# Attention units of a fused attention, feed-forward and expert kernel: one plain float32 form, two heads per tile

## The chip, the cores and the metric

The kernel runs on one core of a Trainium2 chip. The metric is the device time of one execution in microseconds. In three runs the kernel before took 502.41, 504.73 and 507.37 us, median 504.73.

## The reference

Three layers follow each other.

1. A recurrent attention over 768 tokens, for 2 batches and 8 heads of 48 features. For every token `t`: `y = r_t (state + (u k_t) v_t)`, then `state = w * state + k_t v_t`, with a decay `w` (0.85 to 0.95) per head and feature.
2. A feed-forward over all 1536 tokens of 384 features: `elu(x @ w_in) @ w_out`, hidden width 2048; `w_in` and `w_out` come as float64.
3. A mixture of 8 experts: argmax of `x @ w_gate` picks an expert, the softmax weight of the choice scales it; up to 384 tokens per expert, each through `relu(x @ w1) @ w2` with 1024 hidden features.

Everything is compared in float32, so products are either made in plain float32 or from operands split into a high and a low float32r part (three products).

## The kernel before, in words

**Attention.** Tokens are cut into chunks of 128. A *unit* is one chunk of four heads: 24 units, numbered `u`; the halves of the heads alternate, so the state that unit `u` leaves is read by unit `u + 2`, and the last chunk of a batch leaves none. Inside a unit the recurrence becomes products: scores `k^T r` with powers of the decay multiplied into `r` and `k` (`decay_r` L290, `decay_k` L306), a mask that keeps the earlier tokens and puts the bonus of `u` on the diagonal (`bonus` L317 and L318, `diagonal` L322 and L324, `mask` L378), the result `y` from values and masked scores and from the state and `r` (`out`), and the state's update from scaled keys and values (`state`, `carry`). All products of attention are recorded under the helper's line 263.

There are two forms of a unit. Units 0 to 9 (`N_FULL = 10`) are *plain*: products of float32 operands, the tile of `r` and `k` has 48 rows and four heads side by side, a state product per head with a second product that decays the old state, and `out` lets two heads use the lower and two the upper columns of the array at the same time. The high part of `y` is copied by ScalarE (L451); the low part is left in PSUM by a product that takes the high part off, a step later, and copied by ScalarE too (`late_y`, L462 and L463). The state is carried by a copy of ScalarE (L411). Units 10 to 23 are *split*: `r`, `k`, values, scaled keys, masked scores and state are each divided into a high part (a cast by ScalarE) and a low part (a subtraction, all in the helper `sub`, L259, mostly on VectorE); the scores come in two halves that VectorE adds (`sum`, L374).

**Feed-forward.** A *pair* `q` (0 to 47) is two 128-wide hidden blocks of a group of 256 tokens: 18 products into the hidden blocks (`ff_in`, L490), ELU in steps of ScalarE and VectorE, a split, and 18 products out (`ff_out`, L529), two pairs later. The float64 weights are converted in thirds by VectorE (L203, L206, L209), cast by ScalarE (L221), and their low parts subtracted by GpSimd or VectorE (L225). The table `FILL` says how many thirds go where, for `q` from -10 to 10.

**Order.** One call of `half` is one step: the products of pair `q` and half of a unit's work. The first half of a unit has the scores and the mask, the second the result, the state and the carry. Steps run from `q = -10` to 37 with units 0 to 23, in program order on each engine from `q = 9` on (`manual_schedule`); before that a planner orders the instructions by estimated costs. Units 0 to 3 lie ahead of pair 0, units 5 to 9 beside pairs 0 to 9, units 10 to 23 beside pairs 10 to 37. `prep` makes ready the next unit in four stages. `Route` (L588 and what follows) finds the experts of a finished group and borrows the banks of the scores. From `q = 38` on there is no attention, and the experts' weights are loaded into its memory.

**Queues.** Loads of units (L85, L88), of weights, and most of the packing of `y` into the feed-forward's input (L472, two or five transfers per unit) are issued by SP in program order; a load waits for its buffer.

## Time and profile before

| | |
|---|---|
| runs | 502.41, 504.73, 507.37 us |
| span of the profiled execution | 502.5 us (first to last instruction; its own time is not listed apart from the runs) |
| TensorE busy | 449.2 us, 89% |
| VectorE busy | 363.7 us, 72% |
| ScalarE busy | 247.4 us, 49% |
| GpSimd busy | 227.1 us, 45% |
| DMA | 74.29 MB, mean 148 GB/s |
| pair 0 begins | 52.05 us |
| pair 10 begins | 120.02 us |
| pair 38 begins | 295.01 us |

Busy time is an average over stages with different limits. TensorE's products are pipelined, so the records of two neighbours overlap; the time between two starts is the price of a product, not its duration. A plain float32 product leaves two records. In the names of engines PE is TensorE, PEld its weight loads, DVE VectorE, ACT ScalarE, POOL GpSimd, SP SyncE.

### The profile page before, as it was taken

Reading aid. Unit: us, or ns where it says so; the run is one execution under the profiler, and the core shown is the slowest. Engines: PE = TensorE matmul, PEld = TensorE weight load, DVE = VectorE, ACT = ScalarE, POOL = GpSimd, SP = SyncE. Lnnn points to the kernel's source line nnn. Section 1 sums busy time; section 2 is a strip of 40 time slices with the busy share of each in tenths; the row PEclk is TensorE's granted clock in tenths of the full one; section 3 lists DMA queues with packets and bytes.
Section 4 is the critical chain, followed back from the end, with each engine's and each line's share of the span. In section 5 each row is a group of like instructions: output and inputs, shape, how many; then the busy total and the mean of one; then the engine's idle time right before and its main releaser. Section 6 shows DMA issues by size and latency. Waiting matters only on the chain. (4 is left out here: it accounts for less than half of the span.)

```text
span 502.5 us, 9335 instructions
## 1 busy us (share of the span) xinstructions
PE 449.2 (89%) x3646; PEld 432.0 (86%) x3646; DVE 363.7 (72%) x546; ACT 247.4 (49%) x430; POOL 227.1 (45%) x227
## 2 busy tenths in 40 slices
PE   2876996989998989889889999998999999999991
PEld 2554995989998989888889999997999999999991
DVE  7999799995788888888888853555656555755410
ACT  1222543546546655566456646654564655556310
POOL 8587475684477656676566442242110111011011
PEclk9875797799998999999999999998999999999997
DMA  8792555646643452222231028142646656662001
GB/s 225 224 329 78 164 200 181 192 126 218 211 140 101 151 183 87 77 85 90 69 93 43 18 64 313 64 157 97 210 162 235 254 194 233 222 238 97 31 26 30
DMA packets 26693, 74.29 MB, mean 148 GB/s; under 512 B 4098, under 2 KB 12702, under 8 KB 26640
## 3 DMA queue, kind: packets, MB, share of 16 engines
q1 hardware_dynamic: 24352, 68.27, 41.4%
q0 software_dynamic: 1792, 4.75, 2.6%
q8 instruction: 30, 0.49, 0.4%
q10 hardware_dynamic: 496, 0.59, 0.4%
q14 instruction: 23, 0.19, 0.2%
HBM read 57.00 MB, written 12.66 MB: 139 GB/s over the span
## 5 line engine op out<-in xcount | busy, mean ns | idle before, releaser
L490 PE MATMUL h<-xT,w 128*128 128x256 f32 x864 | 118.8, 289 | 0.4 <-DMA xT<-yh 0.4
L529 PE MATMUL x<-g,w 128*128 128x256 f32 x864 | 112.4, 284 | 1.1 <-DVE w L225 1.1
L490 PEld LDWEIGHTS h<-xT,w 128*128 128x128 f32 x864 | 110.2, 194 | 0.7 <-DMA xT<-yh 0.6
L529 PEld LDWEIGHTS x<-g,w 128*128 128x128 f32 x864 | 107.1, 192 | 1.8 <-DVE w L225 1.4
L512 POOL TENSOR_TENSOR g<-e,g 128x512 fp32r<-128x512 f32 x43 | 61.4, 1427 | 83.5 <-ACT g L509 83.3
L689 DVE TENSOR_TENSOR w<-raw,w 128x1536 fp32r<-128x1536 f32 x32 | 57.1, 1784 | 34.3 <-ACT w L688 32.1
L263 PE MATMUL h<-dT,w 128*128 128x256 f32 x576 | 73.4, 281 | 0.0
L263 PE MATMUL y<-w,ht 128*128 128x384 f32 x384 | 72.7, 338 | 0.0
L263 PEld LDWEIGHTS h<-dT,w 128*128 128x128 f32 x576 | 72.3, 190 | 0.0
L783 POOL DMA_INDIRECT out<-o,ds x16 | 15.6, 973 | 124.6 <-ACT o L781 122.2
L263 PEld LDWEIGHTS y<-w,ht 128*128 128x128 f32 x384 | 65.7, 188 | 0.0
L754 ACT ACTIVATE ht<-h 128x512 fp32r<-128x512 f32 x32 | 19.1, 598 | 60.1 <-PE h L263 60.0
L755 DVE SCALAR_TENSOR_TENSOR ht<-h,ht 128x512 fp32r<-128x512 f32 x32 | 22.1, 690 | 36.2 <-ACT ht L754 36.2
L688 ACT CAST w<-raw 128x1536 fp32r<-128x1536 f32 x32 | 47.3, 1477 | 0.8 <-DMA raw<-w 0.8
L509 ACT CAST g<-e 128x512 fp32r<-128x512 f32 x48 | 29.8, 620 | 33.3 <-DVE e L505 33.3
L505 DVE SCALAR_TENSOR_TENSOR e<-h,e 128x512 f32<-128x512 f32 x48 | 32.7, 681 | 17.8 <-ACT e L501 17.7
L497 ACT ACTIVATE e<-h 128x512 f32<-128x512 f32 x48 | 28.5, 594 | 14.1 <-PE h L490 13.4
L225 POOL TENSOR_TENSOR w<-f,w 128x768 fp32r<-128x768 f32 x13 | 30.6, 2357 | 10.5 <-ACT w L221 10.5
L324 POOL TENSOR_SCALAR_AFFINE_SELECT am<-dt 128x512 f32<-128x512 f32 x24 | 23.1, 964 | 27.0 <-DVE dt L322 25.2
L501 ACT ACTIVATE e<-e 128x512 f32<-128x512 f32 x48 | 30.4, 632 | 1.4
L221 ACT CAST w<-f 128x768 fp32r<-128x768 f32 x16 | 13.3, 834 | 23.9 <-DVE f L209 23.0
L206 DVE SCALAR_TENSOR_TENSOR f<-raw,f 128x768 uint32<-128x768 uint32 x16 | 23.3, 1458 | 0.1
(169 smaller groups left out, 683.5 us busy)
## 6 DMA issues: line engine op xcount, KB each, us to landing
raw<-w SPq DMA_DIRECT2D x32, 768.0 KB, 5.0
tok<-tok SPq DMA_DIRECT2D x24, 288.0 KB, 4.7
rk<-rkT SPq DMA_DIRECT2D x14, 448.0 KB, 3.6
raw<-w_in SPq DMA_DIRECT2D x8, 768.0 KB, 6.2
raw<-w_out SPq DMA_DIRECT2D x8, 768.0 KB, 4.6
disp<-zrow SPq DMA_DIRECT2D x6, 776.0 KB, 4.7
ds<-disp SPq DMA_DIRECT2D x9, 388.0 KB, 3.1
out<-zrow SPq DMA_DIRECT2D x4, 576.0 KB, 3.7
```

Source lines behind the costliest of these rows:

```text
L206: nc.vector.scalar_tensor_tensor(out=t, in0=high, scalar=0xC0000000, in1=t, op0=ALU.bitwise_and, op1=ALU.bitwise_or)
L225: (nc.vector if n in LO_V else nc.gpsimd).tensor_tensor(out=w[:, 1, o], in0=t.bitcast(F32), in1=w[:, 0, o].bitcast(F32), op=ALU.subtract)
L263: nc.tensor.matmul(out, x, y, start=start and n == 0, stop=stop and n == len(pairs) - 1, skip_group_check=True)
L490: nc.tensor.matmul(h_ps[:, j], win(d, f, a), x[:, :, d, c], start=n == 0, stop=n == 8)
L497: nc.scalar.activation(out=e, in_=hps[q], func=AF.Exp)
L501: nc.scalar.activation(out=elu[q], in_=elu[q], func=AF.Relu, bias=1.0, scale=-1.0)
L505: nc.vector.scalar_tensor_tensor(out=e, in0=hps.pop(q), scalar=0.0, in1=e, op0=ALU.max, op1=ALU.subtract)
L509: nc.scalar.copy(gt[q][:, 0], elu[q])
L512: eng("v" if q in ELO_V else "p").tensor_tensor(out=gt[q][:, 1], in0=elu.pop(q), in1=gt[q][:, 0].bitcast(F32), op=ALU.subtract)
L529: nc.tensor.matmul(o, wout(f, d, a), gg[:, c, j], start=f == 0 and n == 0 and d != 1, stop=f == 15 and n == 2, skip_group_check=True)
L688: nc.scalar.copy(w[:, 0], raw)
L689: low.tensor_tensor(out=w[:, 1], in0=raw, in1=w[:, 0].bitcast(F32), op=ALU.subtract)
```

## The change

There is one form of unit. Its operands are plain float32 throughout. A tile of `r` and `k` has 112 rows: one head in rows 0 to 47, another in rows 64 to 111, two such pairs side by side, so it is 256 columns wide instead of 512. The four score products read their operands from one row half each and write to two banks, one per row half. The state of a pair of heads lies in one tile, a head on either diagonal block; one product per pair makes its update (the blocks off the diagonal are not used), and one product per pair over 112 rows adds state times `r` to `y`. The tables of powers have four columns of 112 rows instead of eight, and the keys' table has the last power in it from the start. The old state is decayed by VectorE when it is carried, with the decay as a scalar per row, instead of by a product. The low part of `y` is a subtraction of VectorE in the same step as its high part, and packing follows at once. `r` and `k` are decayed in place; values are read where they were loaded; the buffers of loads are three deep instead of two. `decay_k` is on GpSimd for units 1 to 8, on VectorE for the others; the bonus is on VectorE for unit 0, on GpSimd for the others. The input of `r` and `k` is laid out by the host to match. Feed-forward, routing and experts are as before, and `FILL` is the same. Comments are gone.

```diff
@@ sizes and engines
-BONUS_V = (0, 3, 5, 7, 8)
-KD_V = (3, 8, 9)
-N_FULL = 10  # first attention units, multiplied in plain float32
+BONUS_V = (0,)
+KD_P = (1, 2, 3, 4, 5, 6, 7, 8)
@@ load_unit
-        n = D if u < N_FULL else KS
-        pool, kw = (first, {"name": f"rk{u}"}) if u < 4 else (att, {"tag": "rk", "name": "rk"})
-        rk_t[u] = pool.tile([n, 2, HH, C], F32, **kw)
-        nc.sync.dma_start(out=rk_t[u], in_=rkT[u, 0:n])
+        pool, kw = (first, {"name": f"rk{u}"}) if u < 4 else (att, {"tag": "rk", "name": "rk", "bufs": 3})
+        rk_t[u] = pool.tile([KS, 2, 2, C], F32, **kw)
+        nc.sync.dma_start(out=rk_t[u], in_=rkT[u])
@@ tables
-    ew = attc.tile([KS, H, C], F32, name="ew")
+    ew = attc.tile([KS, 4, C], F32, name="ew")
+    kp = attc.tile([P, 4, P], F32, name="kp")
+    e2 = first.tile([KS, 4, C], F32, name="e2")
+    for i in range(4):
+        nc.scalar.activation(out=e2[:, i], in_=ew[:, i], func=AF.Copy, scale=sq[:, 7, i:i + 1])
+    kp_ps = ps_tile(psA, "u")[:, 0:4 * KS]
+    for i in range(4):
+        nc.tensor.transpose(kp_ps[:, i * KS:(i + 1) * KS], e2[:, i], ident[0:KS, 0:KS])
+    nc.scalar.copy(kp[:, :, 0:KS], kp_ps.rearrange("p (i d) -> p i d", i=4))
...
@@ class Unit
+        def decay(self, j, on):
+            x = self.rk[:, j]
+            eng(on).tensor_tensor(out=x, in0=x, in1=ew[:, self.i2], op=ALU.mult)
         def decay_r(self):
+            self.decay(0, "v")
         def decay_k(self):
+            self.decay(1, "p" if self.u in KD_P else "v")
-        def split_r(self):
-        def split_k(self):
-        def values(self):
-        def split_kt(self):
...
         def decay_kt(self):
+            if not self.last:
+                k4 = self.tk[:, 1].rearrange("p (m q d) -> p q m d", m=2, q=2)
+                nc.vector.tensor_tensor(out=self.heads(self.kh), in0=k4, in1=self.heads(kp[:, self.i2]), op=ALU.mult)
+        def scores(self):
+            a = bank().rearrange("p (m x) -> p m x", m=2)[:, :, 0:2 * C]
+            self.a_ps = a.rearrange("p m (q t) -> p m q t", q=2)
+            for q in range(2):
+                for m in range(2):
+                    row = slice(64 * m, 64 * m + D)
+                    group(self.a_ps[:, m, q], [(self.rk[row, 1, q], self.rk[row, 0, q])])
-        def sum(self):
-        def split_a(self):
...
         def state(self):
+            self.u_ps = ps_tile(psA, "u")[0:KS, 0:4 * D].rearrange("p (q m d) -> p q m d", q=2, m=2)
+            v4 = self.tk[:, 2].rearrange("p (m q d) -> p q m d", m=2, q=2)
+            for q in range(2):
+                group(self.u_ps[:, q], [(self.kh[:, q, 0:KS], v4[:, q])])
         def carry(self):
+            for m in range(2):
+                row = slice(64 * m, 64 * m + D)
+                st = self.st[row, :, row]
+                if not self.c:
+                    nc.scalar.copy(st, self.u_ps[row, :, m])
+                    continue
+                for q in range(2):
+                    nc.vector.scalar_tensor_tensor(
+                        out=st[:, q], in0=st[:, q], scalar=sq[row, 7, 2 * self.hf + q:2 * self.hf + q + 1],
+                        in1=self.u_ps[row, q, m], op0=ALU.mult, op1=ALU.add)
-        def split_s(self):
         def out(self):
+            v = self.tk[:, 2]
+            if self.c:
+                for q in range(2):
+                    group(y_two[:, q], [(self.st[:, q, 0:KS], self.rk[:, 0, q])], start=q == 0, stop=False)
+            for q in range(2):
+                for m in range(2):
+                    h = 2 * m + q
+                    group(y_two[64 * m:64 * m + D, q], [(v[:, h * D:(h + 1) * D], self.am[:, h])],
+                          start=q == 0 and not self.c)
         def split_y_low(self):
+            nc.vector.tensor_tensor(out=self.yh[:, :, 1], in0=y_two, in1=self.yh[:, :, 0].bitcast(F32),
+                                    op=ALU.subtract)
+            self.pack()
-        def late_y(self):
@@ half, the one form that is left
-        low_y()
-        prep(n + 1, 0 if first else 1)
-        if not first and not ff:
+        if first:
+            prep(n + 1, 0)
+        elif not ff:
             prep(n + 1, 2)
...
         if x and first:
             x.scores()
-            if n - 1 in units:
-                units.pop(n - 1).late_y()
         elif x:
             x.out()
-            if n == 1:
-                key_table()
             x.state()
...
             elu_max(q)
+        if x and not first:
+            units.pop(n).split_y_low()
+        if ff:
             elu_hi(q)
...
             x.carry()
-            x.split_s()
             prep(n + 1, 3)
-    def half_split(q, n, first):
```

## Rows read from the trace of the kernel before

**Rows 1.** slices of the page: VectorE, busy tenths in 40 equal parts.

```profile
DVE  7999799995788888888888853555656555755410
```

**Rows 2.** windows: busy us (x) of PE, PEld, DVE, ACT, POOL; clock, DMA, GB/s.

```profile
0.00:52.00 52.00, 33.01 (x212) 24.09 (x212) 47.39 (x74) 12.35 (x25) 37.07 (x47) 0.77 0.70 213
52.00:120.00 68.00, 61.61 (x507) 57.84 (x506) 62.71 (x72) 31.94 (x62) 43.46 (x26) 0.90 0.56 177
120.00:295.00 175.00, 159.44 (x1475) 155.76 (x1474) 149.66 (x264) 100.89 (x204) 108.65 (x116) 0.99 0.33 105
```

**Rows 3.** TensorE's waits from 120 to 295 us: us in total, times, longest.

```profile
PE a L263 <- DVE kst L259: 7.3, 8, 2.2
PE a L588 <- DVE as L374: 2.7, 3, 1.0
PE a L263 <- ACT xr L591: 2.2, 2, 1.1
```

**Rows 4.** TensorE timeline, split unit: start us, us, instruction, [idle before].

```profile
192.32 0.51 PE L263 MATMUL u<-vh,kh 128*48 128x96 f32 x8
192.67 0.30 PE L263 MATMUL y<-r,st_s 112*48 112x128 f32 x2
...
193.90 1.28 PE L490 MATMUL h<-xT,w 128*128 128x256 f32 x9
195.92 0.71 PE L263 MATMUL a<-r,kst 112*128 112x256 f32 x4 [0.74 <-DVE kst L259]
196.47 1.22 PE L490 MATMUL h<-xT,w 128*128 128x256 f32 x9
```

**Rows 5.** TensorE's timeline, pairs with no attention beside them.

```profile
307.81 2.31 PE L490 MATMUL h<-xT,w 128*128 128x256 f32 x18
309.96 2.27 PE L529 MATMUL x<-g,w 128*128 128x256 f32 x18
312.06 2.31 PE L490 MATMUL h<-xT,w 128*128 128x256 f32 x18
```

**Rows 6.** TensorE's timeline, scores, result and state of plain units.

```profile
95.61 1.05 PE L263 MATMUL a<-r_f,k_f 128*128 128x128 f32 x8
96.42 1.31 PE L529 MATMUL x<-g,w 128*128 128x256 f32 x9
...
112.97 2.31 PE L490 MATMUL h<-xT,w 128*128 128x256 f32 x18
115.21 0.43 PE L263 MATMUL y<-r_f,st_f 128*48 128x128 f32 x4
...
116.12 0.25 PE L263 MATMUL u<-vh,kh 128*48 128x48 f32 x2
...
117.81 2.37 PE L529 MATMUL x<-g,w 128*128 128x256 f32 x18
```

**Rows 7.** windows, line 259 alone: busy us (x) of DVE and POOL.

```profile
120.00:295.00 175.00, 53.99 (x63) 7.24 (x11) 0.99 0.33 105
```

**Rows 8.** groups by shape, VectorE: busy us, mean ns, idle before.

```profile
L290 DVE TENSOR_TENSOR rk<-rk,ew 112x512 f32<-112x512 f32 x14 | 16.1, 1149 | 0.0
...
L290 DVE TENSOR_TENSOR r_f<-rk,ew 48x512 f32<-48x512 f32 x10 | 10.6, 1066 | 0.0
...
L318 DVE TENSOR_TENSOR tok<-tok 128x192 f32<-128x192 f32 x5 | 3.2, 632 | 0.0
...
L608 DVE SCALAR_TENSOR_TENSOR eq<-lg,mx,io 128x8 f32<-128x8 f32 x12 | 6.5, 578 | 0.2
...
L415 DVE TENSOR_TENSOR st_f<-u,st_f 48x192 f32<-48x192 f32 x8 | 2.8, 350 | 0.8
...
L720 DVE TENSOR_TENSOR dT<-u,dT 128x256 fp32r<-128x256 f32 x2 | 0.8, 420 | 1.0 <-ACT dT L723 1.0
```

**Rows 9.** groups by shape: ScalarE's copies of y and of the state.

```profile
L451 ACT CAST yh<-y 112x256 fp32r<-112x256 f32 x10 | 3.7, 366 | 15.6 <-PE y L263 8.4 <-DMA xT<-yh 7.1
...
L411 ACT COPY st_f<-u 48x192 f32<-48x192 f32 x8 | 2.5, 308 | 8.0 <-PE y L263 5.9 <-PE u L263 2.0
```

More of the change, by code (lines that the diff above doesn't have):

```diff
@@ L160, in bank @@
         return psA.tile([P, 1024], F32, tag="a", name="a")
-    st_s = [attc.tile([KS, HH, D], F32R, name=f"st_s{i}") for i in range(2)]
-    for i in range(2):
-        nc.gpsimd.memset(st_s[i].bitcast(F32), 0.0)
     win_t, wout_t = [], []
@@ L361, in scores @@
-        def scores(self):
-            if self.full:
-                self.a_ps = bank()[:, 0:512].rearrange("p (h t) -> p h t", h=HH)
-                for i in range(HH):
-                    group(self.a_ps[:, i], [(self.k[:, i], self.r[0][:, i])])
-            else:
-                self.a_ps = bank().rearrange("p (h c t) -> p h c t", h=HH, c=2)
-                for i in range(HH):
-                    group(self.a_ps[:, i], [(self.k[:, i], self.r12[:, i])])
-        def sum(self):
-            self.s = att.tile([P, HH, C], F32, tag="am", name="as")
-            nc.scalar.copy(self.s, self.a_ps[:, :, 1])
-            nc.vector.tensor_tensor(out=self.s, in0=self.a_ps[:, :, 0], in1=self.s, op=ALU.add)
@@ L388, in state @@
+        def mask(self):
+            nc.vector.copy_predicated(out=self.am.rearrange("p (m q) t -> p m q t", m=2), mask=mask_b, data=self.a_ps)
         def state(self):
@@ L448, in split_y @@
             pool, kw = (first, {"name": "yh1"}) if self.u == 1 else (att, {"name": "yh"})
-            shape = [KS, 2, 2, C] if self.full else [D, HH, 2, C]
-            self.yh = pool.tile(shape, F32R, tag=kw["name"], bufs=1, **kw)
-            nc.scalar.copy(self.yh[:, :, 0], self.y_ps)
+            self.yh = pool.tile([KS, 2, 2, C], F32R, tag=kw["name"], bufs=1, **kw)
+            nc.scalar.copy(self.yh[:, :, 0], y_two)
         def split_y_low(self):
-            if not self.full:
-                nc.vector.tensor_tensor(out=self.yh[:, :, 1], in0=self.y_ps, in1=self.yh[:, :, 0].bitcast(F32),
-                                        op=ALU.subtract)
-                self.pack()
@@ L459, in late_y @@
-        def late_y(self):
-            if self.full:
-                nc.tensor.matmul(self.y_ps, nident[0:KS, 0:KS], self.yh[:, :, 0], start=False, stop=True, skip_group_check=True)
-                nc.scalar.copy(self.yh[:, :, 1], self.y_ps)
-                self.pack()
+            nc.vector.tensor_tensor(out=self.yh[:, :, 1], in0=y_two, in1=self.yh[:, :, 0].bitcast(F32),
+                                    op=ALU.subtract)
+            self.pack()
         def pack(self):
@@ L911, in half @@
             x.carry()
-            x.split_s()
-            prep(n + 1, 3)
-        fill(q, 2)
-    def half_split(q, n, first):
-        x = units[n]
-        while pending:
-            split_bits(*pending.pop(0))
-        low_y()
-        if not first:
-            prep(n + 1, 2)
-        fill(q, 0)
-        if first:
-            ff_in(q, range(1))
-            x.scores()
-            if n - 1 in units and units[n - 1].full:
-                units.pop(n - 1).late_y()
-            x.sum()
-            ff_in(q, range(1, 2))
-            elu_exp(q)
-            elu_min(q)
-            x.mask()
-            fill(q, 1)
-            elu_max(q)
-            x.split_a()
-            elu_hi(q)
-            ff_out(q - LAG)
-            finish(q)
-            prep(n + 1, 0)
-        else:
-            ff_in(q, range(2))
-            elu_exp(q)
-            elu_min(q)
-            ff_out(q - LAG)
-            finish(q)
-            x.state()
-            elu_max(q)
-            x.out()
-            x.carry()
-            elu_hi(q)
-            ypend.append(x)
-        route_steps(q)
-        elu_lo(q)
-        if not first:
-            x.split_s()
             prep(n + 1, 3)
@@ L988, in rwkv_moe_kernel @@
                 init_out(q - INIT[1])
-        low_y()
         att.release()
```

218 lines of the change are left out of this document (36 added, 182 removed).

## Prediction

> **What bounds the kernel now.** I read the page's slices first [rows 1]: over the first half of the span VectorE stands at 7 to 9 tenths, so it may bound there though TensorE is the busier engine in total. Stages must then be read apart, and three stretches do that [rows 2]: 0 to 52 us (before the first feed-forward product), 52 to 120 us (pairs 0 to 9, with plain attention units) and 120 to 295 us (pairs 10 to 37, the fourteen split units 10 to 23). In the first, VectorE works 47.4 of 52 us and TensorE 33.0: VectorE bounds it, with the conversion of the float64 weights. In the second both are near full (62.7 and 61.6 of 68). In the third TensorE works 159.4 of 175 us, so it stands idle for 15.6, and VectorE has 149.7: the two are tied. The waits of TensorE in that stretch [rows 3] name the tie: 7.3 us before the scores for the low part of the keys, 2.7 us of routing products that want the bank from which VectorE still adds the two halves of the scores, 2.2 us of scores that want the bank back from the routing. The first two are steps of splitting. After 295 us no attention is left, and the change touches nothing; a pair alone takes 312.06 − 307.81 = 4.25 us [rows 5].
>
> **The change, part by part.** It is costed by stretch against the profiled span of 502.5 us. The runs shown are 502.41, 504.73 and 507.37 us, so next to nothing lies around the span, and it is 2.2 us under their median, which I add at the end.
>
> *TensorE, a unit of 120 to 295 us.* A split unit today [rows 4]: state product 192.67 − 192.32 = 0.35 us, result 193.90 − 192.67 = 1.23, scores 196.47 − 195.92 = 0.55; 2.1 together. Prices of plain float32 come from units 0 to 9 [rows 6], where every product is two records. Scores, full width: 96.42 − 95.61 = 0.81 us for eight records, 0.101 each. Result, with two halves of the columns at work at once: 116.12 − 115.21 = 0.91 us for sixteen, 0.057 each. State: 117.81 − 116.12 = 1.69 us for sixteen, 0.106 each, though they are only 48 columns wide: a record costs about 0.1 us whatever its width, unless two halves run side by side.
>
> The new unit has four score products in two row halves (eight records), two products of state and r over 112 rows (four), four of values and masked scores in two column halves (eight), and two state products, one per pair (four). At these rates: scores 8 × 0.057 = 0.46 if the row halves overlap as the column halves do, 0.81 if not; result 4 × 0.106 + 8 × 0.057 = 0.88; state 0.42. No row of before shows row halves. I take 0.46, as the column halves are the same division turned round, and keep 0.81. Going from the whole array to halves costs 0.09: the pair's 18 products ahead of the plain result take 115.21 − 112.97 = 2.24 us [rows 6], and 309.96 − 307.81 = 2.15 with no such product behind them [rows 5]. The row halves of the scores add two such changes to a unit, 0.2 us. The Trainium skill ("TensorEngine Tiling (Array Packing)", Key Properties) says that a change of the tiling mode drains TensorE, which speaks against this change; the trace agrees with its 0.09. By that rule alone, with all four changes of a unit counted as new, fourteen units would cost some 3 us more than in my sum.
>
> A unit: 0.46 + 0.88 + 0.42 + 0.2 = 1.96 us against 2.1; with scores that do not overlap and twice the changes of mode, 2.5. Some units lack a state product or an incoming state, on both sides. Over fourteen units the bounds are −3 and +8 us; I take +1, between them but near the first.
>
> *The waits of 120 to 295 us.* The splits vanish: line 259 alone holds 54.0 us of VectorE there [rows 7], and the fourteen sums of the score halves go too. The decay of r falls from 512 columns (1.15 us) to 256, so 0.42 to 0.57: the 256-wide subtraction, or half of the 512-wide decay [rows 8]. VectorE gains the decay of k at the same price, the low part of y stays and is 256 wide (0.42), and where a chunk has gone before, four small products carry the state. One is 48 columns wide: 256 columns take 0.420, 192 take 0.350, so 1.1 ns a column and 0.19 us for 48. The one operation of this kind with a scalar from memory takes 0.58 on eight columns [rows 8], which is the other end. I take 0.25, nearer the first, since the carry has the operands of the 192-wide state sum, and keep 0.58. VectorE then loses over 54 us and gains 14 × 0.5 for k and 32 × 0.25 for carries: under 110 us of work in the stretch, no longer a bound. GpSimd loses the key decays and the scaled keys, ScalarE seven copies a unit; both had room. The scores' inputs are ready one unit (some 11 us) ahead, as both decays of unit n are issued during unit n − 1. What is late next? The carry, which stands last in VectorE's order behind the ELU and the low part of y; the next unit of the same heads reads it two units on. The mask has a pair (4.25 us) before its result product. On SP's queue the packing of y goes out half a unit earlier, and the loads behind it have three buffers instead of two. I put 2 us for leftovers, 0 to 5 as bounds. The granted clock of 0.99 [rows 2] gives back 0.01 × 175 = 1.7 us where waits had lowered it.
>
> Stretch: 159.4 − 1.7 + 1 + 2 = 160.7, so 14.3 us gained. Bounds: 159.4 − 1.7 − 3 = 154.7 (20.3 gained) and 159.4 + 8 + 5 = 172.4 (2.6 gained).
>
> *0 to 120 us.* VectorE is the bound, so a ledger in its durations [rows 8]. Out: ten decays of r at 1.07, three of k of the same shape (3.2), and four of the five bonus pairs that it held at 2 × 0.63 (5.0): 18.9. In: eleven decays of r and three of k at 0.42 to 0.57 (5.9 to 8.0), ten low parts of y at 0.42 (4.2), 32 carries at 0.19 to 0.58 (6.1 to 18.6): 16.2 to 30.8, and about 19 with carries at 0.25. So nothing is gained or lost, between −3 and +12. GpSimd gets the bonus pairs and shorter key decays. TensorE saves 3.41 − 1.96 = 1.45 us a unit, 7 us over units 5 to 9, of which a full VectorE lets little through; the low part of y needs no product any more. I take 2 us gained, between 8 gained and 10 lost. The smaller tables and the wider loads (112 rows for 48) lie beside the conversion; without that cover they would cost a microsecond or two at the start.
>
> Sum: 502.5 − 14.3 − 2 + 2.2 = **488 us**.
>
> **The rivals.**
> (a) TensorE's saving comes through in the front too, and the overlap is as good as can be: 18 us from the middle and 6.5 from the front give 480 us. For it: TensorE is at 61.6 of 68 us between 52 and 120. Against: VectorE is fuller.
> (b) The carries cost 0.58 each, and VectorE's front grows by some 10 us: 502.5 − 14.3 + 9 + 2.2 = 499 us, at the edge of no change. For it: the one row with a scalar from memory. Against: that is more than 192 columns take, so the row may hold more than the scalar.
> (c) Slower: a wait moves onto the saturated engine. Today ScalarE carries the plain states and takes y out, and it idles for that, 8.0 us before line 411 and 15.6 before line 451 [rows 9], at no cost. Now VectorE, in its order, stands behind TensorE's state product for the carry and behind ScalarE's copy for the low part, with the weight conversion and the next unit's decays queued behind it, and TensorE waits for those weights. If all 23.6 us land on VectorE before 120 us, the front loses 23.6 less the 2: 502.5 − 14.3 + 21.6 + 2.2 = 512 us. It decides from some 16 us of such waits on. Against it: the low part stands behind the ELU's maximum of the same pair, which needs two steps of ScalarE first, by when the result product (0.88 us) is over; and before the first pair conversion steps can stand between.
> (d) The row halves do not overlap: 14 × 0.35 = 5 us, 493 us, inside the forecast's own range.
>
> **How the numbers follow.** Forecast with (d) 0.69, own range 480 to 496; (a) 0.12; (b) 0.11; (c) 0.08. About 1% (5 us) is what can be told from no change here. Faster by more: the forecast, (a) and 0.01 of (b), 0.82; within: the rest of (b), 0.10; slower: (c), 0.08. For eight in ten the range takes (a) down to 476, for its bounds, and (b) up to 500; it leaves out (c) and the far ends of the bounds.
>
> **What would show it.** Right: scores that wait for no VectorE subtraction; a stretch of pairs 10 to 37 near 161 us with TensorE busy nearly throughout; about 0.5 us from the first score record of a unit to the product after the last; carries of 0.2 to 0.3 us. Wrong: score records 0.1 us apart; VectorE idle before 120 us, put down to TensorE's state or ScalarE's copy of y, and TensorE waiting for converted weights; pair 10 starting later than 120 us.

## The result, and the profile after

The changed kernel takes 481.75 us (median of four runs, 480.77 to 482.51), beside 504.77 us for the kernel before in the same set: ratio 0.954, 95% interval 0.949 to 0.960. Its profiled execution took 482.16 us, its span 480.4 us, so 1.7 us lie around the span. Pair 0 begins at 47.70 us, pair 10 at 115.40, pair 38 at 273.38. Where the time came from, by the same stretches as in [rows 2]:

| stretch | before | after | gained | predicted |
|---|---|---|---|---|
| start to pair 0 | 52.05 | 47.70 | 4.35 | } 2 |
| pair 0 to pair 10 | 67.97 | 67.70 | 0.27 | } |
| pair 10 to pair 38 | 174.99 | 157.98 | 17.01 | 14.3 |
| pair 38 to the end | 207.49 | 207.02 | 0.47 | 0 |
| span | 502.5 | 480.4 | 22.1 | 16.3 |

The slices of VectorE in the page of the kernel after, which answer to [rows 1]:

```profile
DVE  5799999997443465547643333646755655656410
```

The 7 to 9 tenths now last ten slices (120 us); after that it is 3 to 7. The windows of the first three stretches of the kernel after: busy us (and instructions) of PE, PEld, DVE, ACT and POOL, then the granted clock, the DMA share and GB/s.

```profile
0.00:47.70 47.70, 25.50 (x132) 18.67 (x133) 38.57 (x81) 11.00 (x22) 32.71 (x48) 1.00 0.72 232
47.70:115.40 67.70, 55.10 (x437) 51.35 (x436) 65.00 (x89) 27.42 (x47) 40.35 (x29) 0.92 0.52 170
115.40:273.38 157.98, 157.98 (x1386) 149.82 (x1385) 83.11 (x221) 63.24 (x119) 69.68 (x83) 1.00 0.33 103
```

The third line is the change's main yield: TensorE is busy 157.98 of 157.98 us, and VectorE, 149.66 us in the stretch before [rows 2], has 83.11. The waits of [rows 3] have no successor: the list of TensorE's waits is empty there. In the second line it is the other way round. TensorE's work fell by 6.5 us (61.61 to 55.10), the stretch by 0.27, and VectorE has 65.00 of 67.70. What TensorE saved it now waits; its waits from 47 to 116 us (engine, what it waits with and the line, what it waits for: us in total, times, longest):

```profile
PE h L374 <- DVE e L389: 4.2, 1, 4.2
PE x L413 <- POOL w L210: 4.0, 1, 4.0
PE y L248 <- DVE am L304: 2.8, 3, 2.0
PE x L413 <- ACT w L206: 1.6, 1, 1.6
```

These sum to 12.6 us, the whole of 67.70 − 55.10: an ELU maximum of pair 1 behind the weight conversion, the low and the high part of a weight piece (piece 12), and masks.

TensorE's timeline of a unit in the third stretch, which answers to [rows 4] (start us, us, instruction):

```profile
185.25 0.71 PE L248 MATMUL a<-rk 48*128 48x128 f32 x8
185.89 2.37 PE L413 MATMUL x<-g,w 128*128 128x256 f32 x18
...
190.26 0.60 PE L248 MATMUL y<-rk,st_f 112*112 112x128 f32 x4
190.79 0.65 PE L248 MATMUL y<-am,tok 128*48 128x128 f32 x8
191.36 0.63 PE L248 MATMUL u<-tok,kh_f 128*112 128x96 f32 x4
191.78 2.35 PE L413 MATMUL x<-g,w 128*128 128x256 f32 x18
```

From start to start: scores 0.64 us, state times r 0.53, values times masked scores 0.57, state 0.42; together 2.16. No line carries an idle time in brackets. The groups of VectorE that the change added, of the whole span (busy us, mean ns, idle before), answer to [rows 8]:

```profile
L263 DVE TENSOR_TENSOR rk<-rk,ew 112x256 f32<-112x256 f32 x40 | 25.6, 669 | 1.8 <-DMA rk<-rkT 1.8
...
L325 DVE SCALAR_TENSOR_TENSOR st_f<-st_f,sq,u 48x48 f32<-48x48 f32 x64 | 14.3, 259 | 0.3
...
L347 DVE TENSOR_TENSOR yh<-y,yh 112x256 fp32r<-112x256 f32 x24 | 9.9, 414 | 1.3 <-ACT yh L344 1.2
```

The carry costs 259 ns and idles for 0.3 us in all, the low part of `y` 414 ns and 1.3 us: the wait that could have moved onto VectorE did not come.

### The profile page after: what moved, and what is told of

It reads as the page before. It is cut to its first block, busy times and chain, and to the rows that moved or that the text cites. A ratio compares the mean times of both kernels' runs of the same rounds, so it can differ in the third digit from the quotient of the medians.

```text
span 480.4 us, 8754 instructions
## 1 busy us (share of the span) xinstructions
PE 433.9 (90%) x3406; PEld 414.2 (86%) x3406; DVE 289.8 (60%) x526; ACT 202.8 (42%) x324; POOL 179.1 (37%) x197
## 5 line engine op out<-in xcount | busy, mean ns | idle before, releaser
L413 PE MATMUL x<-g,w 128*128 128x256 f32 x864 | 115.0, 287 | 5.6 <-POOL w L210 4.0
L374 PE MATMUL h<-xT,w 128*128 128x256 f32 x864 | 115.0, 288 | 4.2 <-DVE e L389 4.2
L374 PEld LDWEIGHTS h<-xT,w 128*128 128x128 f32 x864 | 109.0, 195 | 4.6 <-DVE e L389 4.4
L396 POOL TENSOR_TENSOR g<-e,g 128x512 fp32r<-128x512 f32 x43 | 56.6, 1316 | 113.5 <-ACT g L393 113.4
L667 POOL DMA_INDIRECT out<-o,ds x16 | 15.6, 972 | 124.8 <-ACT o L665 122.4
L639 DVE SCALAR_TENSOR_TENSOR ht<-h,ht 128x512 fp32r<-128x512 f32 x32 | 22.1, 689 | 35.8 <-ACT ht L638 35.8
L210 POOL TENSOR_TENSOR w<-f,w 128x768 fp32r<-128x768 f32 x13 | 26.5, 2041 | 18.6 <-ACT w L206 18.6
L263 DVE TENSOR_TENSOR rk<-rk,ew 112x256 f32<-112x256 f32 x40 | 25.6, 669 | 1.8 <-DMA rk<-rkT 1.8
L248 PE MATMUL a<-rk 48*128 48x128 f32 x192 | 20.2, 337 | 6.2 <-DVE rk L263 6.2
```

The costliest lines, as they stand in the source:

```text
L210: (nc.vector if n in LO_V else nc.gpsimd).tensor_tensor(out=w[:, 1, o], in0=t.bitcast(F32), in1=w[:, 0, o].bitcast(F32), op=ALU.subtract)
L248: nc.tensor.matmul(out, x, y, start=start and n == 0, stop=stop and n == len(pairs) - 1, skip_group_check=True)
L263: eng(on).tensor_tensor(out=x, in0=x, in1=ew[:, self.i2], op=ALU.mult)
L374: nc.tensor.matmul(h_ps[:, j], win(d, f, a), x[:, :, d, c], start=n == 0, stop=n == 8)
L396: eng("v" if q in ELO_V else "p").tensor_tensor(out=gt[q][:, 1], in0=elu.pop(q), in1=gt[q][:, 0].bitcast(F32), op=ALU.subtract)
L413: nc.tensor.matmul(o, wout(f, d, a), gg[:, c, j], start=f == 0 and n == 0 and d != 1, stop=f == 15 and n == 2, skip_group_check=True)
```

## The experiments

All times in us: where pairs begin, from TensorE's timeline of one profiled execution each, and the median of the timed runs with its ratio to the kernel before.

| kernel | pair 0 at | pair 0 to 10 | 10 to 38 | 38 to end | span | median | ratio, 95% |
|---|---|---|---|---|---|---|---|
| after | 47.70 | 67.70 | 157.98 | 207.02 | 480.4 | 481.75 | 0.949 to 0.960 |
| 1 load | 46.28 | 67.72 | 174.48 | 205.42 | 493.9 | 495.79 | 0.976 to 0.988 |
| 2 late inputs | 46.56 | 67.24 | 165.31 | 206.89 | 486.0 | 486.65 | 0.958 to 0.970 |
| 3 both | 46.04 | 68.07 | 195.68 | 205.51 | 515.3 | 516.75 | 1.017 to 1.030 |
| 4 old plain form | 49.90 | 67.92 | 170.33 | 206.65 | 494.8 | 497.43 | 0.981 to 0.992 |
| 5 other order | 45.94 | 67.60 | 158.08 | 205.78 | 477.4 | 478.36 | 0.942 to 0.954 |
| 6 state by head | 46.56 | 68.80 | 156.25 | 206.89 | 478.5 | 478.66 | 0.942 to 0.956 |
| 7 low part of piece 12 | 46.44 | 66.50 | 157.98 | 206.88 | 477.8 | 479.33 | 0.945 to 0.956 |
| 8 less load | 46.45 | 67.45 | 159.88 | 206.92 | 480.7 | 481.52 | 0.945 to 0.953 |
| 9 after, once more | 47.80 | 67.43 | 157.98 | 205.69 | 478.9 | 480.21 | 0.943 to 0.949 |
| 10 halves throughout | 46.60 | 67.19 | 155.99 | 205.92 | 475.7 | 477.76 | 0.936 to 0.946 |
| 11 other filling | 46.97 | 67.58 | 155.99 | 206.86 | 477.4 | 478.44 | 0.939 to 0.945 |
| 12 one row half | 47.18 | 67.79 | 164.14 | 205.99 | 485.1 | 486.78 | one run |

A reading aid: the kernel after and its repetition (9) agree to 0.01 us in the middle stretch, and differ by 1.3 us from pair 38 to the end. So what an edit does to the middle can be read to a tenth of a microsecond, while the start of pair 0 scatters by 2 us among kernels whose front is nearly the same.

**4, old plain form.** The kernel before, with all 24 units in the old plain form: the splits go, the new tiling does not come.

```diff
-N_FULL = 10
+N_FULL = 24
-        low_y()
+        units.pop(NU - 1).late_y()
```

> The kernel before with all 24 units in its own plain form (four heads of 48 rows side by side, a state product and a decay product per head, low part of y left by a product), the last low part taken before attention's memory is freed: the half of the change that drops the splits, without the new tiling. Theory 'TensorE': a plain unit of the old form takes TensorE 0.81 + 0.91 + 1.69 + 0.13 = 3.5 us and some 0.3 for changes of mode against 2.1 of a split one, so the stretch of pairs 10 to 37 becomes 28 x 4.25 + 6 + 14 x 3.8 minus what units without a state save (4 x 1.7 + 2 x 0.4), 170 to 175 us without a wait, and the time is 500 to 506 us, no change from before. Rival 'splits alone': dropping the splits gives the gain by itself, 482 to 490 us.

Measured: 497.43 us, the middle 170.33: in the stretch the theory's number, at its low end; the time is 2.6 us under its range, mostly because pair 0 began 2.15 us earlier than in the kernel before. The window of the middle, and one unit in TensorE's timeline of this kernel:

```profile
117.82:288.15 170.33, 170.33 (x1554) 163.95 (x1553) 61.98 (x158) 71.42 (x152) 83.35 (x94) 1.00 0.30 90
```

```profile
190.98 1.05 PE L263 MATMUL a<-r_f,k_f 128*128 128x128 f32 x8
191.79 0.36 PE L462 MATMUL y<-yh,nident 112*112 112x256 f32 x1
191.99 2.29 PE L529 MATMUL x<-g,w 128*128 128x256 f32 x18
...
196.37 0.42 PE L263 MATMUL y<-r_f,st_f 128*48 128x128 f32 x4
...
197.28 0.25 PE L263 MATMUL u<-vh,kh 128*48 128x48 f32 x2
...
198.97 1.21 PE L529 MATMUL x<-g,w 128*128 128x256 f32 x8
```

TensorE is busy all of the 170.33 us, with VectorE at 62. So taking the splits away empties the 15.6 us of waits by itself, but the old plain products bring 10.9 us of work (170.33 − 159.44), and 4.7 us are left. A unit costs 0.81 + 0.20 + 0.91 + 1.69 = 3.61 us here and 2.16 in the kernel after. The new tiling is worth the other 170.33 − 157.98 = 12.35 us: added up over the stretch from start to start, the units' products take 40.98 us here and 27.57 in the kernel after, 13.41 less, and the feed-forward's products beside them 1.06 more (123.51 and 124.57).

The state product is dear here for another reason than the prediction gave. Its sixteen records go in turns over 128 rows (`vh`, `kh`) and over 48 rows (`st_f`, `wd`, the decay of the old state). Two units of this stretch have no old state; one of them, up to the next start:

```profile
149.07 0.52 PE L263 MATMUL u<-vh,kh 128*48 128x48 f32 x8
149.52 0.74 PE L529 MATMUL x<-g,w 128*128 128x256 f32 x4
```

Eight records of 48 columns take 0.45 us, 0.056 each, in one half of the columns. So the 0.106 of [rows 6] is not the price of a record of 48 columns as such. How much the turns add and how much the 48-row products cost was not isolated.

**1, load.** The kernel after, with seven products of 128x512 more per unit on VectorE in units 10 to 23, on a tile that nobody reads.

```diff
+            for _ in range(k):
+                nc.vector.tensor_tensor(out=junk, in0=junk, in1=junk, op=ALU.mult)
# k = 3 behind the diagonal, 1 ahead of and 1 behind the mask, 2 behind the carry
```

> The changed kernel with seven idle 512-wide float32 products a unit added to VectorE for units 10 to 23 (three where the split of r, k and values stood, two around the mask, two behind the carry), which nothing reads: 14 x 7 x 0.68 = 67 us, the work that VectorE lost between pair 10 and pair 38 (149.7 to 83.1 us). Theory 'chain' (TensorE waited because the low parts were made just ahead of the scores): VectorE is again at 150 of 158 us, but the scores' inputs are ready a unit ahead, so the stretch of pairs 10 to 37 stays within 3 us of 158.0 and the time within 481 to 486. Rival 'load' (VectorE as the bound, whatever its place in the chain): the stretch returns to 168 to 175 us and the time to 492 to 500.

The window of the middle, and the added group in it:

```profile
114.00:288.48 174.48, 160.01 (x1386) 150.27 (x1385) 162.10 (x318) 61.58 (x119) 80.19 (x82) 1.00 0.29 92
```

```profile
L151 DVE TENSOR_TENSOR junk<-junk 128x512 f32<-128x512 f32 x95 | 87.7, 923 | 1.6
```

The load came out heavier than meant: 923 ns an operation on average instead of the 680 by which I had sized it. VectorE then has 162.1 us of work, more than the 158 us that TensorE needs. The stretch grows by 16.5 us, as the rival "load" had it; but that says what an overload does, not what the load of the kernel before did. Experiment 8 has less.

**8, less load.** Five operations a unit: 2, 1, 1 and 1 in the same places.

> The changed kernel with five idle 512-wide products a unit on VectorE instead of the seven of e1. There each took 0.92 us, not 0.68, so VectorE had 162 us of work in the stretch of pairs 10 to 37; five make about 147 us, as before the change (149.7). If VectorE's share alone set the waits, TensorE idles as it did before the change, 12 to 16 us, the stretch is 170 to 175 us and the time 491 to 495. If the waits grow only when VectorE comes near the whole stretch, and the old waits needed the low parts' place ahead of the scores as well, the stretch is 160 to 166 us and the time 480 to 488.

The middle in the windows of this kernel:

```profile
113.90:273.78 159.88, 158.79 (x1387) 150.10 (x1385) 141.00 (x291) 62.40 (x119) 81.29 (x83) 1.00 0.32 100
```

VectorE's share is now 141.0 / 159.9 = 0.88, about that of the kernel before (149.7 / 175 = 0.86), and the stretch grows by 1.9 us, not by 15. A share of 86% did not by itself make the old waits. But waits lengthen the stretch that a share is taken of. Set against the work of TensorE, the load is 141.0 / 158 = 0.89 here, 162.1 / 158 = 1.03 in experiment 1, and it was 149.7 / 159.4 = 0.94 in the kernel before, which lies between and was not run. A straight line between the two experiments gives some 8 us at 149.7 us of work, an estimate: fullness alone may have made up to half of the old 15.6 us, and is not shown to have made all.

**2, late inputs.** Both decays of units 11 and later are issued at the start of the unit's own first half, ahead of its scores, and no longer during the unit before. VectorE's work stays as it is.

```diff
-            x.decay_k()
-            x.decay_r()
+            if u < 11:
+                x.decay_k()
+                x.decay_r()
...
         if first:
+            if x and n >= 11:
+                x.decay_k()
+                x.decay_r()
             prep(n + 1, 0)
```

> The changed kernel with both decays of units 11 to 23 issued at the start of the unit's own first half, one pair's 18 products (2.15 us) ahead of the scores, instead of a unit ahead. 'Chain': a wait before the scores comes back only if the two decays (0.84 us unhindered, up to 2 us beside GpSimd) and what stands before them on VectorE take longer than 2.15 us; with VectorE half idle I expect 0 to 3 us in the stretch, 481 to 485 us. 'Load': no change at all, 481 to 483.

Windows, VectorE's timeline and TensorE's timeline around one unit of this kernel:

```profile
113.80:279.11 165.31, 158.76 (x1386) 150.14 (x1385) 82.39 (x221) 63.07 (x118) 69.05 (x83) 1.00 0.31 98
```

```profile
182.78 0.90 DVE L325 SCALAR_TENSOR_TENSOR st_f<-st_f,sq,u 48x48 f32<-48x48 f32 x4
183.69 1.98 DVE L288 TENSOR_TENSOR kh_f<-tok,kp 128x192 f32<-128x192 f32 x1
185.59 1.55 DVE L263 TENSOR_TENSOR rk<-rk,ew 112x256 f32<-112x256 f32 x2
```

```profile
187.24 0.71 PE L248 MATMUL a<-rk 48*128 48x128 f32 x8 [0.93 <-PE h L374]
```

The middle grows by 7.3 us, more than the 0 to 3 expected, though VectorE is at 82.4 of 165.3, half empty. The scores start 0.1 us after the decay ends (185.59 + 1.55 = 187.14). They do so in eleven of the thirteen units whose decays were moved, and 6.55 of the 7.3 us are TensorE's idle time just before these scores. The bracket names TensorE's own product as the releaser; two engines' timelines laid side by side show that it was the decay, which stands in VectorE's order behind four carries and the scaled keys. Lateness costs something at an idle engine, but only half of the old 15.6 us.

**3, both.** Experiment 1's seven operations and experiment 2's order together.

> Both edits together: VectorE as full as before the change, and the scores' inputs made just ahead of them. 'Chain' and 'load' both expect waits before the scores. 'Chain': most of the loss needs both, 8 to 15 us in the stretch of pairs 10 to 37, 489 to 497 us, and more than e1 and e2 add up to. 'Load': as much as e1 alone.

The middle in the windows, and TensorE's largest wait there:

```profile
114.11:309.79 195.68, 170.55 (x1386) 161.44 (x1385) 157.13 (x319) 63.52 (x119) 78.28 (x83) 0.93 0.26 82
```

```profile
PE a L255 <- issue: 21.0, 10, 3.5
```

The middle grows by 37.7 us, more than the 16.5 and 7.3 apart, and more than the 8 to 15 that the theory expected. The view names no releaser, but in all thirteen units the scores start 0.10 to 0.15 us after VectorE's decay ends, so they stand behind everything that VectorE has in its order; and 12 us of it are TensorE's own records (170.55 for 158) at a clock of 0.93. In size it overshoots the kernel before. What the three runs show is that fullness and lateness together cost more than their sum; the kernel before had both (a chain of splits ahead of the scores, on an engine at 86%). How its 15.6 us divide between them was not settled, as neither the load alone nor the two together were run at its load. My theory that the place in the chain alone made the waits falls with experiments 1 and 2. Its rival, the load alone, is weakened by 8 and not refuted.

**5, other order.** Scores with the row halves one after the other instead of in turns.

```diff
-            for q in range(2):
-                for m in range(2):
+            for m in range(2):
+                for q in range(2):
```

> The changed kernel with the four score products in another order: both of the first row half, then both of the second, so that neighbours use the same half. If the halves overlap only when they alternate, eight records take 0.8 to 1.0 us instead of 0.64 from the first score to the product after the last, 0.2 to 0.35 us a unit, 3 to 5 us over pairs 10 to 37, 484 to 487 us. If the halves do not overlap in the changed kernel either, or overlap in any order, the unit stays at 0.64 us and the time at 481 to 483.

The scores of one unit, and the product behind them, in TensorE's timeline:

```profile
194.39 0.72 PE L248 MATMUL a<-rk 48*128 48x128 f32 x8
195.04 2.37 PE L413 MATMUL x<-g,w 128*128 128x256 f32 x18
```

0.65 us instead of 0.64, and the stretch 158.08: the order in which the halves are issued makes no difference. The time, 478.36 us, is under the 481 to 483 expected because pair 0 began at 45.94. That left open whether the halves overlap at all.

**12, one row half.** All four score products read rows 0 to 47. The scores of the heads in rows 64 to 111 are left out, and the others made twice; the instructions are as many and as wide.

```diff
-                    row = slice(64 * m, 64 * m + D)
+                    row = slice(0, D)
```

> The changed kernel with all four score products read from rows 0 to 47, so that none can run beside one of the other row half (the scores of the heads in rows 64 to 111 are left out and those of the others computed twice). If the row halves overlap in the changed kernel, eight records take 0.85 to 1.05 us instead of 0.64 from the first score to the product after the last, 0.2 to 0.4 us for each of fourteen units, and the stretch of pairs 10 to 37 is 161 to 164 us. If records of 48 rows are cheap by themselves, nothing changes: 158.0 us.

The same place in TensorE's timeline of this kernel:

```profile
187.46 1.16 PE L248 MATMUL a<-rk 48*128 48x128 f32 x8
188.54 2.37 PE L413 MATMUL x<-g,w 128*128 128x256 f32 x18
```

The same eight records take 188.54 − 187.46 = 1.08 us instead of 0.64, and the stretch grows by 6.16 us = 14 × 0.44. So the overlap of the row halves is real, whatever the order. A record in one row half alone (1.08 / 8 = 0.135 us) is even dearer than one over the whole array (0.101, [rows 6]), so without the overlap the scores would have cost more than the 0.81 us that rival (d) took. The Trainium skill ("TensorEngine Tiling (Array Packing)", Key Properties) says that tiles work independently, so that their loads and products can run in parallel; the 1.08 and 0.64 us agree.

**6, state by head.** The state product of a pair of heads (112 rows of output, 96 columns, off-diagonal blocks unused) becomes one product of 48 columns for each head, each into its own column half.

```diff
-            for q in range(2):
-                group(self.u_ps[:, q], [(self.kh[:, q, 0:KS], v4[:, q])])
+            for m in range(2):
+                row = slice(64 * m, 64 * m + D)
+                for q in range(2):
+                    group(self.u_ps[row, q, m], [(self.kh[:, q, row], v4[:, q, m])])
```

> The changed kernel with a state product per head instead of one per pair: four products of 48 columns by 48 in the place of two of 112 by 96, in an order in which neighbours use the same columns. Eight records at 0.106 us are 0.85 us against 0.41: 0.44 us for each of the ten units with a state between pairs 10 and 37, 4 us there. Theory on the front: pair 0 began 4.35 us earlier because conversion ran 1.9 us ahead and because the state product of unit 4, which stood between the conversion's last product and pair 0, shrank from 2.6 us to 0.25; then pair 0 begins 0 to 1.5 us later here than 47.7 us (half the records come back, if they stand there at all). In all 485 to 489 us. Rival: records of 48 columns side by side overlap in any order, no change, 481 to 483 us.

Result and state of one unit in TensorE's timeline:

```profile
190.02 0.64 PE L248 MATMUL y<-am,tok 128*48 128x128 f32 x8
190.49 0.38 PE L248 MATMUL u<-tok,kh_f 128*48 128x48 f32 x8
190.81 2.39 PE L415 MATMUL x<-g,w 128*128 128x256 f32 x18
```

My theory here was wrong: the halves overlap, as the rival had it, and more, for the rival had said no change. Twice the records take 0.32 us instead of 0.42, as 48 columns in two column halves cost 0.04 us a record; my 0.106 was the price of another product (experiment 4). The products ahead of them end sooner as well, 0.47 us for 0.57, with no change of tiling between. That it is what stands behind them that counts is shown inside this kernel: of the fourteen units ten have a state product and 0.47 us, and the four without one, where the feed-forward follows, keep 0.57. One of the four:

```profile
268.80 0.64 PE L248 MATMUL y<-am,tok 128*48 128x128 f32 x8
269.37 2.40 PE L415 MATMUL x<-g,w 128*128 128x256 f32 x18
```

The stretch falls by 1.73 us to 156.25. The other half of the expectation, on the front, did not come: pair 0 began at 46.56 us, before 47.7 and not after it. The conversion's first turning product came 1.5 us earlier than in the kernel after; from there to pair 0 the time grew from 3.62 to 3.99 us, so the records that came back do stand there.

**7, low part of piece 12.** The low part of that weight piece, a wait of 4.0 us above, goes from GpSimd to VectorE.

```diff
-LO_V = (5, 14)
+LO_V = (5, 12, 14)
```

> The changed kernel with the low part of weight piece 12 on VectorE instead of GpSimd. In the changed kernel TensorE waits 1.6 and 4.0 us near 90 us for this piece, whose low part stands on GpSimd behind bonus products of attention. VectorE does it in 0.95 us, GpSimd in 2.5 after a wait. If that wait is a loss of its own, pair 10 begins 2 to 4 us earlier than 115.4 and the time falls to 478 to 480 us; if VectorE's order makes another product late instead, the time stays at 480 to 484.

TensorE's largest wait in pairs 0 to 9 of this kernel:

```profile
PE y L248 <- DVE am L304: 4.7, 3, 2.3
```

The 4.0 us are gone from the list, 1.9 of them stand before the masks again (2.8 to 4.7), and pairs 0 to 9 take 66.50 us instead of 67.70 and 67.43. Pair 10 begins 2.5 us earlier, at 112.94, as expected if the wait was a loss of its own; but 1.3 of that lies ahead of pair 0, where nothing was changed, and with the same edit in experiment 10 pairs 0 to 9 take 67.19. So a gain of the edit is not shown.

**9, after, once more,** beside 10 and 11.

> The changed kernel itself once more, beside the next two, as the mark for them: 479 to 483 us, the stretch of pairs 10 to 37 at 158.0 us; the start of pair 0 may lie 2 us either way, as it did between runs that do not differ there.

It took 480.21 us (479.91 to 480.73).

**10, halves throughout.** Experiments 6 and 7, and state times `r` by head into column halves too, so that all three groups of the second half of a unit have one tiling.

```diff
-                    group(y_two[:, q], [(self.st[:, q, 0:KS], self.rk[:, 0, q])], start=q == 0, stop=False)
+                    for m in range(2):
+                        row = slice(64 * m, 64 * m + D)
+                        group(y_two[row, q], [(self.st[:, q, row], self.rk[:, 0, q])], start=q == 0, stop=False)
```

> The changed kernel with a state product per head (as in e6, where the unit's state took 0.32 instead of 0.41 us and the result that follows it no longer gave way to another mode of the array), the product of state and r cut into two column halves (112 rows, 48 columns each, blocks off the diagonal left out) so that the whole result is made in column halves, and the low part of weight piece 12 on VectorE (as in e7). The state-times-r product falls from 0.53 to about 0.45 us if its halves overlap, one change of mode less a unit: the stretch falls from 158.0 to 155 to 156 us, the front by a microsecond, the time to 476 to 478. If the column halves do not overlap over 112 rows, they cost 0.85 us, and the stretch is 159 to 161.

The second half of one unit in TensorE's timeline:

```profile
187.91 0.64 PE L248 MATMUL y<-rk,st_f 112*48 112x128 f32 x8
188.39 0.61 PE L248 MATMUL y<-am,tok 128*48 128x128 f32 x8
188.82 0.38 PE L248 MATMUL u<-tok,kh_f 128*48 128x48 f32 x8
189.14 2.37 PE L417 MATMUL x<-g,w 128*128 128x256 f32 x18
```

0.48 + 0.43 + 0.32 = 1.23 us for what took 1.52, and a middle of 155.99 us, 2.0 less. Of these, 1.73 are experiment 6's. Halving state times `r` brings only the other 0.26: that group falls from 0.53 to 0.48 us, but the 18 products ahead of it, behind which the halves now begin, rise by 0.09 (2.24 to 2.33, and 2.15 to 2.24). In time 477.76 us (474.91 to 479.62) beside 480.21: the fastest median of all kernels here, and all its four runs lie below all four of 9, though the intervals of the two ratios overlap. Its gain on the kernel after is in the middle, the part that repeats.

**11, other filling.** Experiment 10 with four thirds of the weight conversion later, two from the end of pair 0 to the end of pair 2 and two from the end of pair 5 to the steps behind it, to get VectorE to the ELU maximum of pair 1 sooner. Only the entries of `FILL` that differ are shown.

```diff
- 0: (0, 0, 5),
+ 0: (0, 0, 3),
- 2: (0, 1, 0),
+ 2: (0, 1, 2),
- 5: (1, 1, 2),
+ 5: (1, 1, 0),
```

> As e10, with four thirds of the weight conversion moved later (FILL: 3 instead of 5 at the end of pair 0, 2 more at the end of pair 2, 2 fewer at the end of pair 5). In the changed kernel TensorE waits 4.2 us near 60 us for the ELU's maximum of pair 1, which stands on VectorE behind conversion steps. If those steps only stand in the wrong place, that wait goes and pair 10 begins 2 to 4 us earlier after pair 0 (66 us to 62 to 64), 473 to 476 us in all. If VectorE is full in any order, another wait takes its place and the front stays at 66 us.

478.44 us, pairs 0 to 9 at 67.58: no gain. The wait of 4.2 us is gone from the list; in its place TensorE waits 5.3 us for masks (3.8 in experiment 10) and 3.1 for what the profile does not name. So in this order, as the rival had it, another wait takes its place; one other order does not show that none is better.

## Why the prediction was right, step by step

It said 488 us and the kernel took 481.75: faster, inside the range of 476 to 500 and near the lower end of the forecast's own.

**The bound of the middle: right.** The waits were steps of splitting. Without splits they are gone in either tiling (experiment 4: none in 170.33 us; after: none in 157.98). VectorE has 83.1 us there, foreseen as under 110.

**The leftover waits: 2 us taken, 0 measured.** This is most of the middle's surplus of 2.7 us. The carry, named as late next, is no cause of any wait.

**TensorE's work: +1 us taken, about +0.2 measured, by luck: a unit was mis-sized.** The sum 159.44 − 1.7 + 1 had 158.7; the stretch has 157.98. A full unit costs 2.25 us by the prediction's count, not 1.96. Scores have 0.64 where 0.46 and one change were taken, and the change into the halves lies outside that, in the 18 products ahead (2.24 us for 2.15): 0.73 for 0.66. The result has 1.10 for 0.88. State times r has 0.53 where four records make 0.42, values times scores 0.57 where eight make 0.46: 0.11 each, at the two places where the tiling goes from the whole array to column halves and back. I had counted such changes at the scores alone. The rule weighed in the prediction, from the Trainium skill ("TensorEngine Tiling (Array Packing)", Key Properties), was right in this: with all four changes counted it asked for some 3 us more, and 14 × 0.2 = 2.8. Experiment 6 shows the price of leaving the halves, 0.10 us, inside one kernel, and experiment 10 that the price of entering them, 0.09, moves to the products ahead. The kernel before shows that the change of tiling alone need not cost this: its split units go from the feed-forward into products on 48 columns of the array too (`128*48` in [rows 4]), and the 18 products ahead take 2.10 to 2.11 us, as with none behind ([rows 5]: 2.10). The groups that paid here were all plain float32.

The state's 0.42 is right in number, but its source was not: the 0.106 behind it is the price of sixteen records in turns (experiment 4). Four records over 112 rows and 96 columns happen to cost 0.103 each.

That the stretch did not come out longer is due to the +1, which I had put above the unit's own sum, 14 × (1.96 − 2.1) = −2. Added up over the stretch without idle time, the units' products took 28.23 us before and 27.57 after, 0.7 less. The row halves, which no row of before showed, do overlap (experiment 12), so rival (d) is out; but eight records took 0.64 us and not the 0.5 of the sign that I had named.

**The carries: right.** 259 ns for 250; rival (b) with 0.58 is out. The low part of `y`: 414 ns for 0.42. The decays of `r` and `k`: 669 ns on average for 0.42 to 0.57, too cheap: the 18 of the 40 that ran while GpSimd was idle took 409 to 424 ns, the others up to 2.2 us.

**The front: the size wrong, 4.6 us for 2, and the place too.** I let 2 us through from TensorE's savings in units 5 to 9. Those savings came (6.5 us) and went into waits, with VectorE at 65.0 of 67.7 us; the stretch gained 0.27. That part of the argument, that a full VectorE lets little through, was right, only stricter than I took it. The gain is ahead of pair 0, where I had costed no saving, so the front came out on the right side in part by luck. TensorE's timelines of the kernel before and after, at that place:

```profile
45.96 2.07 PE L263 MATMUL h<-f,idwg 128*128 128x512 f32 x2 [3.29 <-DVE f L209]
...
49.46 0.40 PE L263 MATMUL u<-vh,kh 128*48 128x48 f32 x2
...
52.05 2.93 PE L490 MATMUL h<-xT,w 128*128 128x256 f32 x12
```

```profile
44.08 2.08 PE L248 MATMUL h<-f,idwg 128*128 128x512 f32 x2 [1.96 <-DVE f L194]
...
47.45 0.55 PE L248 MATMUL u<-tok,kh_f 128*112 128x96 f32 x2
47.70 4.51 PE L374 MATMUL h<-xT,w 128*128 128x256 f32 x27
```

The first product that turns weights around starts 1.88 us earlier, as VectorE's conversion gets there sooner, and ahead of pair 0 stood a state product of sixteen records, 52.05 − 49.46 = 2.59 us, of which 0.25 is left; two of its four records now come after pair 0 has begun, at 54.24. That makes 1.88 + 2.34 = 4.2 of the 4.35. Not all of it is the change. The granted clock under those sixteen records was 0.50, the lower of TensorE's two levels (1.2 GHz); in experiment 4, with the same products at the same place, it was 1.00 and they took 1.74 us, so 0.85 us is the clock of that one execution. And the conversion's first turning product, at 45.96 before, is at 44.92 in experiment 4 and at 42.3 to 44.2 with the new form. With the old form pair 0 starts at 49.90 and 52.05, with the new one at 45.9 to 47.8 in twelve executions: the difference is beyond the scatter, its size is known only as some 2 to 6 us, and no experiment that holds all else divides it.

VectorE's ledger held on its own terms: from the start to pair 10 the decays, bonus pairs, low parts and carries nearly cancel. But VectorE's busy time fell from 47.39 + 62.71 = 110.10 us to 38.57 + 65.00 = 103.57. The ledger had left out the splits of unit 10, which the kernel before made ready ahead of pair 10 (2.8 us), and that other operations took less time: the conversion's 48 thirds 58.6 us before and 56.8 after, the negated identity (one operation) 1.6 and 0.2.

**Rival (c): out.** It needed some 16 us of waits of VectorE for ScalarE's copy of `y` or TensorE's state product. Up to pair 10 the first is 1.2 us and the second too small to be listed:

```profile
DVE dt L279 <- POOL tok L275: 3.4, 3, 1.8
...
DVE yh L347 <- ACT yh L344: 1.2, 2, 1.0
```

The first line, a wait for GpSimd's bonus, is one that I had not named. Of the 23.6 us that the rival moved, 7.1 were waits for a DMA by the row itself [rows 9]. What did come is the reverse: up to 48 us TensorE waits 5.3 us for VectorE's low part of `y`; its last wait ahead of pair 0 is still for the conversion (1.96 us, above).

**Rival (a)** gave 480 us, nearer in number than the forecast, but its two reasons did not hold: the overlap is not as good as could be (0.64 us for 0.46), and TensorE's saving in pairs 0 to 9 did not come through.

**The median.** I took 2.2 us from span to median, as if next to nothing lay around the span and the execution profiled were the fastest. In the runs here 1.7 to 1.8 us lie around the span. For the kernel before 504.77 − 502.5 = 2.3 us came out all the same; for the kernel after it is 1.3, as its median is 0.4 under its profiled execution.

## What to carry to other kernels

Before splitting float32 operands to save products, or undoing it, cost both engines by the stretch: here dropping the splits was worth 4.7 us alone, since the plain products ate what the waits gave back, and only the denser tiling made it 17. Where an engine that feeds the array is in program order, look at how full it is and how late the inputs stand in its order together; here a load alone cost 2 us (141 us of work beside TensorE's 158) or 16.5 (162 us), lateness alone 7 at a half empty engine, and lateness with the larger load 38. A saving on an engine that is not the bound becomes a wait (6.5 us in pairs 0 to 9), so look for the gain where the engine's work stands alone on the path, as the last state product ahead of pair 0 did; what that one brought is read from timelines and not isolated.

## What the runs showed of the hardware that was not expected

- A plain float32 product over the whole array costs about 0.1 us a record at 96 (0.41 / 4) and at 128 columns (0.101, [rows 6]). At 48 columns in one column half it was 0.056 (0.45 / 8, experiment 4), with two column halves in turns 0.04 (0.32 / 8, experiment 6), and at 128 columns with two column halves 0.06. So "about 0.1 us whatever its width" does not hold at 48 columns.
- Eight records in column halves cost 0.10 us more when the feed-forward follows than when another product in halves does (0.57 and 0.47, experiment 6).
- The halves overlap whatever the order of issue: 0.64 and 0.65 us for eight records, against 1.08 in one half.
- The same operation of VectorE has two prices. Experiment 1's 128x512 product from 150 to 180 us, min/median/max in ns:

```profile
L151 DVE TENSOR_TENSOR junk<-junk x17: 672/691/1681, 149.1 to 178.7; 128x512 f32<-128x512 f32 x17
```

  So the mean of 923 ns is made of many at 0.69 us and some at 1.7. The trace tells them apart by GpSimd: of all 98, the 37 during which GpSimd was idle took 671 to 693 ns, and every one above 700 ns (up to 2117) lay beside work of GpSimd. The decays of 256 columns in the kernel after do the same: 409 to 424 ns with GpSimd idle, up to 2207 beside it. Not every operation beside GpSimd was slowed, and no run took GpSimd's work away.
